# First loads over two queues, a finer start order and the z broadcast through DMA transposes

## Chip, cores and metric

The kernel runs on one core of a Trainium2 chip. The metric is the device time of one execution in microseconds (us); of several executions the median is taken. Engines are named as in the profile: PE is TensorE (PEld its weight loads), DVE VectorE, ACT ScalarE, POOL GpSimd, SP SyncE.

## What is computed

x has 2048 tokens of D = 640 bf16 values. Two branches are mixed by a gate per token:

```python
g = sigmoid((x * gate_w).sum(-1, keepdims=True))
# A: linear attention, 32 heads of 20
q, k, v = heads(x @ wqkv)
pq, pk = phi(q), phi(k)            # phi(t) = where(t > 0, t + 1, exp(t)) + 1e-6
kv = einsum("bhsd,bhse->bhde", pk, v)
z = einsum("bhsd->bhd", pk)        # sum over all tokens
o = einsum("bhqd,bhde->bhqe", pq, kv) / (einsum("bhqd,bhd->bhq", pq, z)[..., None] + 1e-6)
a = merge(o) @ wo
# B: token-shift mixer, then MLP (F = 1728)
h = gelu(layernorm(x) @ w1)        # its four column quarters are shifted by 1, -1, 2, -2 tokens
x1 = x + shifted(h) @ w2
b = x1 + gelu(layernorm(x1) @ w3) @ w4
out = g * a + (1 - g) * b
```

## The kernel before

**Tiles and stages.** The 2048 tokens are 16 tiles of 128; D is five blocks of 128. A matmul needs the contracted dimension on partitions, so x is held as x_tok (tokens on partitions) and as xT (columns of x on partitions). The stages, in TensorE's order: a warm-up of matmuls on constants; q = x wq and k = x wk for the tiles, with phi on ACT and DVE behind them; products of pk and x (GT), from which kv follows; W1, W2 (mixer); W3 with the attention output tiles; W4 and the output. A q or k tile is, for each of five slices k of the weight, a matmul of 512 columns and one of 128 (130 for k, which carries a column of ones and gate_w), into a pair of PSUM banks. I call the two matmuls of tile t and slice k a step (t, k).

**Start.** SyncE's queue issues nearly all first loads one after the other, in program order (lines 676 to 704): x tiles 0 and 1, wq slice 0, x tile 2, wq slices 1 to 4, wk slice 0, x tile 3, wk slices 1 to 4, x tile 4, then DMA transposes of x tiles from 3 on (`x_turn`) and the rest of x. ACT's queue issues only a small load that touches rows of wqkv ("touch") and gate_w. x tiles 0, 1, 2 are turned by TensorE (`t_x`, line 763): five transposes against an identity into one PSUM bank, then one DVE copy of 128x640 to xT. Tile 2's turn also brings gate_w onto partitions with a matmul of 5 columns. The identity is made on GpSimd (line 668) after a memset of ones_c (line 659).

TensorE starts with WARM = 3200 columns of matmuls on ones, turns tiles 0 and 1, adds WARM2 = 512 columns, and goes into `q_three` (line 896), in which the steps of q tiles 0, 1, 2 are interleaved by a list written by hand; (None, None) there is a warm-up of 256 columns and (2, None) the turn of tile 2. `k_two` does the same with k tiles 0 and 1, and from `("k", 2)` on whole tiles follow. `stream` (line 873) emits such a list and takes a pair of banks when a tile's first step comes.

**z.** `z_add` sums pk over the 16 tiles on DVE into zsum (128 partitions x 640), still one partial sum per partition. `zb_group` (line 1025) sums over the partitions and copies the sum to all of them at once: two matmuls with a block of ones as weights (line 600) and zsum as the moving operand, then one DVE copy to zb. `qn_sum` (line 1086) multiplies q tiles by zb for the denominators.

**Order.** Every engine takes its instructions in program order and waits for semaphores that the helper class derives from overlapping tiles. The order of independent pieces ("items") is set by a small planner: each `IT.add(stream, name, duration, function, deps)` is an item with dependences and lags, and `IT.run` repeatedly takes the item that can start first by a cost model kept in the program. So a new item or another modelled cost can move items on all engines. The `ZB` stream's item waits for `("z", 15)` and `("w2", 0)`. On SyncE the DMA transposes of normalised tiles for W1 (`t_xn`, line 849, issued at line 281, sixteen of them), then the loads of w3 and w4 (line 285) follow each other in the same stretch of time.

Of the kernel before, what the change touches and what calls it, by code (L numbers as in the profile page):

```python
# [11 lines left out]
D = 640  # L12
# [404 lines left out]
def _build(nc, A_x, A_wqkv, A_wo, B_w1, B_w2, B_w3, B_w4, gate_w, out, dbg=None, stop=None):  # L417
# [45 lines left out]
    def psb(b, n0, n1):  # L463
        return ps[:, b, :].bitcast(BF16)[:, n0:n1]
# [23 lines left out]
    dnr = pa.alloc("dnr", [128, 2, 4, H], F32)  # L488
    xn = pa.alloc("xn", [128, 3, D], BF16)
# [183 lines left out]
    def dma_in(out_ap, in_ap, key, **kw):  # L673
        return sch.dma("sp", out_ap, in_ap, key, **kw)

    sch.dma("act", junk[0:16, 0, 0:80].rearrange("p (k f) -> p k f", k=KD),
            A_wqkv[:, 0:16].rearrange("(k e r) f -> e r k f", k=KD, r=8)[:, 0, :, :], "touch")
    dma_in(x_tok[:, 0, :], x2[0:128, :], "x0")
    dma_in(x_tok[:, 1, :], x2[128:256, :], "x1")
    def load_wq(k):  # L680
        dma_in(wq[:, k, :], A_wqkv[128 * k:128 * (k + 1), 0:D], "wq%d" % k)

    load_wq(0)
    dma_in(x_tok[:, 2, :], x2[256:384, :], "x2")
    for k in range(1, KD):
        load_wq(k)
    for k in range(KD):
        dma_in(wkg[:, k, 0:D], A_wqkv[128 * k:128 * (k + 1), D:2 * D], "wk%d" % k)
        if k == 0:
            dma_in(x_tok[:, 3, :], x2[384:512, :], "x3")  # L690
# [4 lines left out]
    dma_in(x_tok[:, 4, :], x2[512:640, :], "x4")  # L695
    x_turn(3)
    gwr = xn[:, 1, 0:128]
    dve(lambda e: e.memset(gwr, 0.0), [], [gwr])
    sch.dma("act", xn[0:KD, 1, 0:128], gate_w.rearrange("(k p) -> k p", p=128), "gw")
# [60 lines left out]
    WARM = 3200  # L760
    WARM2 = 512

    def t_x(t):
        b = bank()
        tr_group(b, [x_tok[:, t, 128 * k:128 * (k + 1)] for k in range(KD)])
        src = psb(b, 0, D).rearrange("p (k c) -> p k c", k=KD)
        dst = xT[:, :, 128 * t:128 * (t + 1)]
        if t == 2:
            mm_group(ps[:, b, 448:448 + KD], [(gwr, ident[:, 0:KD])])
        copy(dve, dst, src)  # L770
        if t == 2:
            copy(dve, wkg[:, :, D + 1:D + 2], ps[:, b, 448:448 + KD].rearrange("p (k o) -> p k o", o=1))
# [100 lines left out]
    def stream(order, w, n2, done):  # L873
        bs = {}
        for t, k in order:
# [6 lines left out]
            if k == 0:  # L882
                bs[t] = pair()
                bank_hold.update((bs[t], bs[t] + 1))
# [27 lines left out]
    for i in range(2):  # L912
        addA(("tx", i), 0.28, lambda i=i: t_x(i))
# [414 lines left out]
```

## Time and profile before

| | us |
|---|---|
| median of 8 runs | 260.49 |
| lowest and highest | 260.14, 261.64 |
| profiled execution | 260.24 |
| its span in the profile | 259.0 |
| TensorE busy in it | 256.0 |
| ACT / DVE / POOL busy | 106.5 / 152.1 / 93.5 |
| first real matmul (L889) starts | 5.15 |
| last matmuls end | about 257 |

The span is what the hardware profiler saw of one execution, from its first to its last event. In the groups, "busy" counts every instruction from its start to its modelled end; matmuls are pipelined, so their lengths overlap and 99% busy is not the share of peak. An instruction's line can be that of a helper (line 600 issues most matmuls), so tiles tell more than lines. A wait is put down to the engine whose semaphore came last. "From issue to landing" is the time from the start of a DMA's issue on its queue to its last semaphore step.

### The profile page before, as it was taken

Reading aid. Unit: us, or ns where it says so; the run is one execution under the profiler, and the core shown is the slowest. Engines: PE = TensorE matmul, PEld = TensorE weight load, DVE = VectorE, ACT = ScalarE, POOL = GpSimd, SP = SyncE. Lnnn points to the kernel's source line nnn. Section 1 sums busy time; section 2 is a strip of 40 time slices with the busy share of each in tenths; the row PEclk is TensorE's granted clock in tenths of the full one; section 3 lists DMA queues with packets and bytes.
Section 4 is the critical chain, followed back from the end, with each engine's and each line's share of the span. In section 5 each row is a group of like instructions: output and inputs, shape, how many; then the busy total and the mean of one; then the engine's idle time right before and its main releaser. Section 6 shows DMA issues by size and latency. Waiting matters only on the chain.

```text
span 259.0 us, 4292 instructions
## 1 busy us (share of the span) xinstructions
PE 256.0 (99%) x1685; PEld 132.3 (51%) x1685; DVE 152.1 (59%) x288; ACT 106.5 (41%) x216; POOL 93.5 (36%) x151
## 2 busy tenths in 40 slices
PE   8999999999999999999999999999999999999996
PEld 4555555544454554555445445554455544456453
DVE  1587877899903799998998407992033410143233
ACT  1496777751365766676853240005500045100000
POOL 4013995969962029666914202320011110021001
DMA  6965888682666982552726650232000020000211
GB/s 178 277 131 151 191 172 147 183 128 49 104 127 115 399 284 45 60 101 52 104 50 122 124 70 0 49 90 66 0 3 0 3 101 0 0 3 1 104 51 51
DMA packets 51406, 25.16 MB, mean 97 GB/s; under 512 B 42766, under 2 KB 49975, under 8 KB 51386
## 3 DMA queue, kind: packets, MB, share of 16 engines
q1 hardware_dynamic: 50000, 21.47, 36.6%
q0 software_dynamic: 1136, 3.28, 5.4%
q8 instruction: 13, 0.21, 0.3%
q10 hardware_dynamic: 250, 0.14, 0.2%
q14 instruction: 7, 0.06, 0.1%
HBM read 12.05 MB, written 2.62 MB: 57 GB/s over the span
## 4 chain that ended last, share of the span: by engine, by line
PE 97%; DMA 1%; DVE 1%; SPq 0%; issue 0%
PE ps L600 61%; PE ps L1167 22%; PE ps L796 8%; PE ps L889 2%; DMA wq<-in_A_wqkv_dram 1%; PE ps L1079 1%; PE ps L1149 1%; PE ps L890 1%; DVE x_tok L639 0%; PE ps L969 0%; PE ps L998 0%; SPq L285 0%; DVE xT L665 0%; PE ps L1146 0%; PE ps L611 0%
## 5 line engine op out<-in xcount | busy, mean ns | idle before, releaser
L600 PE MATMUL ps<-xnT,w 128*128 128x512 bf16 x360 | 81.5, 379 | 0.0
L1167 PE MATMUL ps<-w,h2T 128*128 128x512 bf16 (+1 forms) x416 | 58.8, 299 | 0.0
L656 ACT ACTIVATE h2T<-ps 128x512 bf16<-128x512 f32 x52 | 30.5, 598 | 67.5 <-PE ps L600 67.5
L600 PEld LDWEIGHTS ps<-xnT,w 128*128 128x128 bf16 x360 | 34.1, 98 | 38.5 <-issue 0.9
L639 DVE SCALAR_TENSOR_TENSOR x_tok<-ps,stg,abx 128x512 bf16<-128x512 f32 (+1 forms) x32 | 17.3, 550 | 61.5 <-PE ps L1167 61.5
L622 POOL TENSOR_SCALAR abx<-x_tok,stg 128x640 f32<-128x640 bf16 x16 | 15.3, 956 | 98.9 <-DVE x_tok L639 94.9
L1167 PEld LDWEIGHTS ps<-w,h2T 128*128 128x128 bf16 x416 | 32.1, 98 | 24.9 <-issue 1.1
L622 POOL TENSOR_SCALAR xn<-x_tok,st 128x640 bf16<-128x640 bf16 x32 | 34.9, 1099 | 13.8 <-DMA xnT<-xn 13.3
L656 ACT ACTIVATE Er<-ps 128x640 bf16<-128x640 f32 x32 | 22.4, 708 | 16.9 <-PE ps L600 7.9
L655 ACT ACTIVATE junk<-x_tok 128x640 bf16<-128x640 bf16 x32 | 23.7, 739 | 3.1 <-DVE x_tok L637 2.6
L600 PE MATMUL ps<-M_sb,pqnT 128*128 128x512 bf16 (+1 forms) x160 | 24.3, 299 | 0.0
L656 ACT ACTIVATE hsT<-ps 128x512 bf16<-128x512 f32 (+1 forms) x32 | 18.9, 593 | 13.1 <-PE ps L600 12.7
L600 PE MATMUL ps<-w,hsT 128*128 128x512 bf16 (+1 forms) x160 | 23.7, 299 | 0.0
L639 DVE SCALAR_TENSOR_TENSOR abx<-ps,stg,abx 128x640 f32<-128x640 f32 x16 | 14.1, 883 | 12.4 <-PE ps L600 11.3
L600 PE MATMUL ps<-wkg,xT 128*128 128x130 bf16 (+1 forms) x140 | 21.4, 299 | 0.0
L600 PE MATMUL ps<-wq,xT 128*128 128x512 bf16 (+1 forms) x130 | 19.8, 299 | 0.0
L600 PEld LDWEIGHTS ps<-w,hsT 128*128 128x128 bf16 x160 | 13.3, 98 | 12.2
L600 PEld LDWEIGHTS ps<-M_sb,pqnT 128*128 128x128 bf16 x160 | 13.2, 98 | 10.9
L796 PE MATMUL ps<-pk_tok,x_tok 128*128 128x512 bf16 x80 | 17.8, 379 | 0.0
L622 DVE TENSOR_SCALAR Er<-Er 128x640 bf16<-128x640 bf16 x32 | 11.7, 366 | 9.4 <-ACT Er L656 9.3
L1108 DVE TENSOR_TENSOR pq_tok<-pq_tok,dnr 128x300 bf16<-128x300 bf16 (+1 forms) x48 | 16.8, 404 | 0.6
L637 DVE SCALAR_TENSOR_TENSOR x_tok<-ps,x_tok 128x640 bf16<-128x640 f32 x16 | 13.1, 820 | 6.8 <-PE ps L600 5.9
(78 smaller groups left out, 227.9 us busy)
## 6 DMA issues: line engine op xcount, KB each, us to landing
w<-in_B_w_dram SPq DMA_DIRECT2D x1, 2160.0 KB, 9.5
w<-in_B_w_dram SPq DMA_DIRECT2D x1, 2080.0 KB, 15.0
out_dram<-x_tok SPq DMA_DIRECT2D x3, 640.0 KB, 3.1
x_tok<-in_A_x_dram SPq DMA_DIRECT2D x2, 640.0 KB, 5.1
w<-in_B_w_dram POOLq DMA_DIRECT2D x8, 160.0 KB, 4.4
x_tok<-in_A_x_dram SPq DMA_DIRECT2D x5, 160.0 KB, 3.3
wq<-in_A_wqkv_dram SPq DMA_DIRECT2D x5, 160.0 KB, 3.4
wkg<-in_A_wqkv_dram SPq DMA_DIRECT2D x5, 160.0 KB, 4.0
```

Source lines behind the costliest of these rows:

```text
L600: ins = e.matmul(out_ap, l, r, start=(i == 0), stop=(i == n - 1))
L622: return engf(lambda e: e.tensor_scalar(out_ap, in_ap, s1, s2, op0, op1), rd, [out_ap], cost=cost)
L637: return dve(lambda e: e.scalar_tensor_tensor(out_ap, in0, scalar, in1, op0, op1, accum_out=accum), rd, [out_ap, accum], cost=cost + 70.0)
L639: return dve(lambda e: e.scalar_tensor_tensor(out_ap, in0, scalar, in1, op0, op1), rd, [out_ap], cost=cost)
L655: return act(lambda e: e.activation(out_ap, in_ap, func, bias=bias, scale=scale, accum_out=accum), rd, wr, cost=cost)
L656: return act(lambda e: e.activation(out_ap, in_ap, func, bias=bias, scale=scale), rd, wr, cost=cost)
L796: ins = e.matmul(o, l, r, start=(t0 + q_ == 0), stop=(t0 + q_ == NT - 1))
L889: e.matmul(ps[:, b, 0:512], l, w[:, k, 0:512], start=(k == 0), stop=(k == KD - 1))
L890: return e.matmul(ps[:, b + 1, 0:n2], l, w[:, k, 512:512 + n2], start=(k == 0), stop=(k == KD - 1))
L1079: ins = e.matmul(o, l, r, start=st, stop=sp)
L1108: dve(lambda e, o=o, i0=i0, i1=i1: e.tensor_tensor(o, i0, i1, ALU.mult), [i0, dnr[:, 1, sd, :]], [o], cost=cost)
L1167: ins = e.matmul(o, l, r, start=False, stop=(i == KFF - 1), skip_group_check=(n0 > 0))
```

## The change

- x tile 0 and wq slice 0 are each loaded in two column parts, one by SyncE's and one by ACT's queue; wq slices 1, 3, 4 and wk slices 1, 3 are issued by ACT, the rest by SyncE. wq slice 0 is now issued before x tile 1. The touch load is gone. gate_w is loaded by GpSimd's queue, ahead of GpSimd's memsets.
- WARM is 2944 columns and WARM2 256; the warm-up of 256 columns inside `q_three` is gone.
- The turn of tiles 0 and 1 is in two parts with a bank and a copy each: block 0, then blocks 1 to 4. Tile 1 is turned inside `q_three`, after step (0, 0); the order of the steps is another, and tile 2 is turned later in it.
- `stream` takes the pairs of banks of all its tiles at its start.
- zb is made without TensorE: a DMA transpose of zsum into zb (`z_turn`), a DVE sum along the free dimension into zc and an ACT copy that spreads zc over zsum (`z_rows`), and a second DMA transpose into zb (`z_back`). The item `("zt",)` waits for `("t1", 7)`, `("zr",)` for the first kv group.

```diff
@@ -486,6 +486,7 @@
     M_sb = pa.alloc("M_sb", [128, KD, D], BF16)
     zb = pa.alloc("zb", [128, D], BF16)
     dnr = pa.alloc("dnr", [128, 2, 4, H], F32)
+    zc = pa.alloc("zc", [128, KD], F32)
     xn = pa.alloc("xn", [128, 3, D], BF16)
     junk = pa.alloc("junk", [128, 1, D], BF16)
     qprod = pa.alloc("qprod", [128, D], F32)
@@ -673,30 +674,39 @@
     def dma_in(out_ap, in_ap, key, **kw):
         return sch.dma("sp", out_ap, in_ap, key, **kw)
 
-    sch.dma("act", junk[0:16, 0, 0:80].rearrange("p (k f) -> p k f", k=KD),
-            A_wqkv[:, 0:16].rearrange("(k e r) f -> e r k f", k=KD, r=8)[:, 0, :, :], "touch")
-    dma_in(x_tok[:, 0, :], x2[0:128, :], "x0")
-    dma_in(x_tok[:, 1, :], x2[128:256, :], "x1")
-    def load_wq(k):
-        dma_in(wq[:, k, :], A_wqkv[128 * k:128 * (k + 1), 0:D], "wq%d" % k)
-
-    load_wq(0)
-    dma_in(x_tok[:, 2, :], x2[256:384, :], "x2")
-    for k in range(1, KD):
-        load_wq(k)
-    for k in range(KD):
-        dma_in(wkg[:, k, 0:D], A_wqkv[128 * k:128 * (k + 1), D:2 * D], "wk%d" % k)
-        if k == 0:
-            dma_in(x_tok[:, 3, :], x2[384:512, :], "x3")
+    def load_x(t):
+        dma_in(x_tok[:, t, :], x2[128 * t:128 * (t + 1), :], "x%d" % t)
+
+    def load_wq(k, queue):
+        sch.dma(queue, wq[:, k, :], A_wqkv[128 * k:128 * (k + 1), 0:D], "wq%d" % k)
+
+    def load_wk(k, queue):
+        sch.dma(queue, wkg[:, k, 0:D], A_wqkv[128 * k:128 * (k + 1), D:2 * D], "wk%d" % k)
 
     def x_turn(t):
         sch.dma("sp", xT[:, :, 128 * t:128 * (t + 1)], x_tok[:, t, :], "trx%d" % (t % 4), transpose=True)
 
-    dma_in(x_tok[:, 4, :], x2[512:640, :], "x4")
-    x_turn(3)
     gwr = xn[:, 1, 0:128]
     dve(lambda e: e.memset(gwr, 0.0), [], [gwr])
-    sch.dma("act", xn[0:KD, 1, 0:128], gate_w.rearrange("(k p) -> k p", p=128), "gw")
+    for n0, n1, queue in ((0, 384, "sp"), (384, D, "act")):
+        sch.dma(queue, x_tok[:, 0, n0:n1], x2[0:128, n0:n1], "x0", group_total=2)
+    for n0, n1, queue in ((0, 320, "sp"), (320, D, "act")):
+        sch.dma(queue, wq[:, 0, n0:n1], A_wqkv[0:128, n0:n1], "wq0", group_total=2)
+    load_x(1)
+    load_wq(1, "act")
+    load_wq(2, "sp")
+    load_wq(3, "act")
+    load_x(2)
+    load_wq(4, "act")
+    load_wk(0, "sp")
+    load_wk(1, "act")
+    load_x(3)
+    load_wk(3, "act")
+    load_wk(2, "sp")
+    load_wk(4, "sp")
+    load_x(4)
+    x_turn(3)
+    sch.dma("pool", xn[0:KD, 1, 0:128], gate_w.rearrange("(k p) -> k p", p=128), "gw")
     for c in range(1, NCH):
         t0 = 5 if c == 1 else 4 * c
         dma_in(x_tok[:, t0:4 * c + 4, :], x2[128 * t0:512 * (c + 1), :].rearrange("(n p) d -> p n d", p=128), "xc%d" % c)
@@ -757,19 +767,18 @@
         assert tags.get((buf, sl)) == what, ("stale ring slot", buf, sl, what, tags.get((buf, sl)))
 
     IT = _Items()
-    WARM = 3200
-    WARM2 = 512
+    WARM = 2944
+    WARM2 = 256
 
     def t_x(t):
-        b = bank()
-        tr_group(b, [x_tok[:, t, 128 * k:128 * (k + 1)] for k in range(KD)])
-        src = psb(b, 0, D).rearrange("p (k c) -> p k c", k=KD)
-        dst = xT[:, :, 128 * t:128 * (t + 1)]
-        if t == 2:
-            mm_group(ps[:, b, 448:448 + KD], [(gwr, ident[:, 0:KD])])
-        copy(dve, dst, src)
-        if t == 2:
-            copy(dve, wkg[:, :, D + 1:D + 2], ps[:, b, 448:448 + KD].rearrange("p (k o) -> p k o", o=1))
+        for k0, k1 in ((0, 1), (1, KD)) if t < 2 else ((0, KD),):
+            b = bank()
+            tr_group(b, [x_tok[:, t, 128 * k:128 * (k + 1)] for k in range(k0, k1)])
+            if t == 2:
+                mm_group(ps[:, b, 448:448 + KD], [(gwr, ident[:, 0:KD])])
+            copy(dve, xT[:, k0:k1, 128 * t:128 * (t + 1)], psb(b, 0, 128 * (k1 - k0)).rearrange("p (k c) -> p k c", k=k1 - k0))
+            if t == 2:
+                copy(dve, wkg[:, :, D + 1:D + 2], ps[:, b, 448:448 + KD].rearrange("p (k o) -> p k o", o=1))
 
     def phi(b, dst, after_exp=None):
         se = slot("E", 3)
@@ -872,6 +881,9 @@
 
     def stream(order, w, n2, done):
         bs = {}
+        for t in sorted({t for t, k in order if k is not None}):
+            bs[t] = pair()
+            bank_hold.update((bs[t], bs[t] + 1))
         for t, k in order:
             if k is None:
                 if t is None:
@@ -879,9 +891,6 @@
                 else:
                     t_x(t)
                 continue
-            if k == 0:
-                bs[t] = pair()
-                bank_hold.update((bs[t], bs[t] + 1))
             b = bs[t]
             l = xT[:, k, 128 * t:128 * (t + 1)]
 
@@ -894,8 +903,8 @@
                 done(t, b)
 
     def q_three():
-        order = [(0, 0), (None, None), (1, 0), (2, None), (0, 1), (1, 1), (2, 0), (0, 2), (1, 2), (2, 1), (0, 3), (0, 4),
-                 (1, 3), (2, 2), (1, 4), (2, 3), (2, 4)]
+        order = [(0, 0), (1, None), (0, 1), (1, 0), (1, 1), (0, 2), (1, 2), (2, None), (0, 3), (1, 3), (0, 4), (2, 0),
+                 (2, 1), (1, 4), (2, 2), (2, 3), (2, 4)]
         stream(order, wq, 128, lambda t, b: phi(b, pq_tok[:, t + 1, :]))
 
     def k_out(t, b):
@@ -909,8 +918,7 @@
         IT.add("A", name, dur, fn, deps)
 
     addA(("warm",), 0.0, lambda: warmup(WARM, 0.834))
-    for i in range(2):
-        addA(("tx", i), 0.28, lambda i=i: t_x(i))
+    addA(("tx", 0), 0.28, lambda: t_x(0))
     addA(("warm", 1), 0.0, lambda: warmup(WARM2, 0.42))
     addA(("q", 2), 4.08, q_three)
     addA(("k", 1), 2.72, k_two)
@@ -1022,18 +1030,27 @@
         for j in range(KD):
             sch.dma("sp", M_sb[60:68, j, :], Mt[8 * j:8 * j + 8, :], "mt", group_total=KD)
 
-    def zb_group():
-        b = pair()
-        mm_group(ps[:, b, 0:512], [(ones_c[:, 0:128], zsum[:, 0:512])])
-        mm_group(ps[:, b + 1, 0:128], [(ones_c[:, 0:128], zsum[:, 512:D])])
-        copy(dve, zb[:, :], psf[:, 512 * b:512 * b + D])
+    zT = zb[:, :].rearrange("p (k n) -> p k n", n=128)
+    zrep = zsum[:, :].rearrange("p (k n) -> p k n", n=128)
+
+    def z_turn():
+        sch.dma("sp", zT, zsum[:, :], "trz", transpose=True)
+
+    def z_rows():
+        dve(lambda e: e.tensor_reduce(zc[:, :], zT, mybir.AxisListType.X, ALU.add), [zT], [zc[:, :]], cost=820.0)
+        activation(zrep, zc[:, :].unsqueeze(2).to_broadcast([128, KD, 128]), ACTF.Copy)
+
+    def z_back():
+        sch.dma("sp", zT, zsum[:, :], "trz", transpose=True)
 
     IT.add("KVF", ("kvt", 1), 0.0, kvt_group, deps=[(("g", KD - 1), 1.0)])
     IT.add("KVF", ("lt", 1), 0.0, lt_evac, deps=[(("kvt", 1), 0.0)])
     IT.add("KVF", ("m", 0), 0.0, m_last, deps=[(("lt", 1), 1.0), (("w1", 2, 2), 0.0)])
     IT.add("KVF", ("m", 1), 0.0, m_first, deps=[(("lt", 1), 1.0), (("w3", 0, 5), 0.0)])
     IT.add("MT", ("mt",), 0.0, m_tail, deps=[(("m", 1), 1.5), (("qt", 2), 0.0)])
-    IT.add("ZB", ("zb",), 0.0, zb_group, deps=[(("z", NT - 1), 1.7), (("w2", 0), 0.0)])
+    IT.add("ZB", ("zt",), 0.0, z_turn, deps=[(("z", NT - 1), 1.7), (("t1", 7), 0.0)])
+    IT.add("ZB", ("zr",), 0.0, z_rows, deps=[(("zt",), 2.6), (("kvt", 1), 0.0)])
+    IT.add("ZB", ("zb",), 0.0, z_back, deps=[(("zr",), 1.5)])
 
     SHIFT = (1, -1, 2, -2)
     PIECES = [[(0, 128, SHIFT[j])] for j in range(4)] + [[(32 * g_, 32 * (g_ + 1), SHIFT[g_]) for g_ in range(4)]]
```

## Prediction

> **What bounds the kernel now.** First the page's parts 1 and 4.
>
> ```profile
> PE 256.0 (99%) x1685; PEld 132.3 (51%) x1685; DVE 152.1 (59%) x288; ACT 106.5 (41%) x216; POOL 93.5 (36%) x151
> ...
> PE 97%; DMA 1%; DVE 1%; SPq 0%; issue 0%
> ```
>
> TensorE is the bound. The share hides the start, so next the waits of its weight loads (us in total, times, longest), in the stretch 5.2 to 257 us:
>
> ```profile
> PEld ps L1149 <- ACT h2T L656: 1.3, 3, 0.4
> ...
> PEld ps L889 <- DMA wq<-in_A_wqkv_dram: 0.6, 1, 0.6
> PEld ps L889 <- DVE xT L665: 0.4, 1, 0.4
> ```
>
> Weight loads run ahead of matmuls, so a wait of theirs need not stop the array: where the load waits on ACT at L1149 the matmuls still follow each other without a hole. Spacing the matmul starts by their columns leaves only two holes after 5 us: before the first real matmul (5.15) and 0.22 us at 6.88. After 6.88 TensorE never stands. So a microsecond saved at the start, or a matmul removed, shortens the run one for one, unless a new hole opens. The chain of waits has the start in order:
>
> ```profile
> 0.79 0.40 SPq L285
> 1.25 0.42 SPq L285
> 1.71 3.39 DMA wq<-in_A_wqkv_dram
> 5.15 0.39 PE ps L889
> ...
> 6.33 0.50 DVE xT L665
> 6.88 0.39 PE ps L889
> ```
>
> The first real matmul waits for wq slice 0, the third load that SyncE issues. TensorE's timeline shows what stands before it:
>
> ```profile
> 0.83 2.83 PE L862 MATMUL ps<-const-bfloat16-1.0 128*128 128x512 bf16 x7 [0.83 <-PEq L1313]
> 3.45 1.27 PE L611 MATMUL ps<-ident,x_tok 128*128 128x128 bf16 x10
> 4.52 0.57 PE L862 MATMUL ps<-const-bfloat16-1.0 128*128 128x512 bf16 x1
> 5.15 0.39 PE L889 MATMUL ps<-wq,xT 128*128 128x512 bf16 x1
> ```
>
> Ten transposes start 0.107 us apart, 4.52 less 3.45; later ones 0.054. The array runs at half pace. The 512-column warm-up matmul takes 0.63 us at half pace and 0.38 at full; the one at 4.52 took 0.57, so it turned fast about three quarters through, near 4.85 us.
>
> **What the Trainium skill says.** "TensorE: Matmul & The Clock Gate", Part 1: the array starts at half clock and goes to full after a busy window of about 3.4 us, whose phase is free. Here it took 0.83 to 4.85, 4.0 us: agrees, and a first matmul before 4.85 is paid double. "DMA: Bandwidth & Descriptors", "Issuing engines are not separate DMA queues": a second issuing engine saves only issue time. Here an issue takes 0.43 us and a landed slice about 0.45 (0.16 MB at the 369 GB/s of the stretch 7.0 to 7.5), so issue is not the limit, and I count mainly on the changed order. The trace doesn't show two full queues at once.
>
> **The change part by part.**
>
> *Loads.* From issue to landing, by window: x tiles 0 and 1 2.4 us, wq slice 0 3.4, x tile 2 and wq slice 1 3.3. So they land at 3.2, 3.65, 5.1, 5.5 and 5.95. A slice should cost 0.45; slice 0 came 1.45 after x tile 1. The stretches 3.0 to 4.0 show only 102 and 138 GB/s with DMA engines 0.7 busy: slow packets. Slice 0 moves ahead of x tile 1: 0.45 earlier, 4.65. What two queues do in the slow spell is not shown: nothing (4.65), or the second fills it so that slice 0 is ready when TensorE is free, about 4.0 (end of its first transposes and warm-up). I take 0.3 earlier, 4.35. Halves cut rows of 1280 bytes to 512 to 768; the trace has 18 ns for 256 bytes and 55 for 1280, so two halves of 640 cost some 64 ns instead of 55: with eight rows per engine, 0.07 us per slice, inside that choice. The touch load (2.3 us, ACT) goes; whether it speeds slice 0 isn't shown, 0 to 0.4 us of loss, taken at 0, kept in the range.
>
> *ACT's queue* issues seven loads, 0.4 us each, from 0.80 to about 4.0; behind them stand the table load (1.28 us, at 1.85 now) and the first Exp, which waits for TensorE until 8.72. Hidden by 3 us.
>
> *gate_w on GpSimd.* Later GpSimd issues take 0.5 to 1.1 us, and this one waits for the VectorE memset (0.88, 0.11). The memset of ones_c and the identity are behind it: identity ready at 1.89 now, then at 2.6 to 3.2. The first transpose comes at 3.24 (next point). Cost 0, at worst 0.1. gate_w itself is needed at x tile 2's turn, after 6.5; GpSimd loads later take 4.4 to 6.8 us at the median, so it is there at about 6 at the latest but for 1 us in the worst case, kept in the range.
>
> *Warm-up.* 256 columns less at half pace: 0.21, transposes from 3.24. Five transposes 0.53, 256 columns 0.21: TensorE is free at 4.0, before slice 0.
>
> *Q order.* Before, from 5.15 to K tile 2 at 12.62 is 7.47 us: 25 steps (640 columns, 0.272 each) 6.80, 256 warm-up columns 0.11, x tile 2's turn and gate matmul 0.34, the hole 0.22. After: 6.80 + 0.34 + x tile 1's turn 0.28 = 7.42, without warm-up and hole (three steps now lie between x tile 2's copy, 0.49, and its use). Starting at 4.35, 0.5 us to the fast clock count half: as if started at 4.60.
> New holes: x tile 1 lands 0.45 after slice 0 (4.80), step (0,0) ends about 4.87: none. wq slice 1 at 5.25, x tile 1's turn ends 5.15: 0.10. Five steps bring it to 6.61; x tile 2 is the fifth slice after wq slice 0, 4.35 + 2.25 = 6.60, or later by the slow spell that wq slice 3 shows now (3.5 to 3.7 us to landing instead of 3.3): 0.15 taken, 0 to 0.6. So K tile 2 starts at 4.60 + 7.42 + 0.25 = 12.27 instead of 12.62: **0.35 us gained**. The split copy of x tiles 0, 1 adds two VectorE instructions of 0.1 to 0.2 us while VectorE idles (3.2 us of waiting there): 0. Pairs of PSUM banks taken up front leave two banks for turns; the copies free these within 0.5 us: 0.
>
> *z.* Two matmuls of 640 columns on ones and zsum go:
>
> ```profile
> L600 PE MATMUL ps<-zsum,ones_c x2: 219/299/379, 83.2 to 83.4; 128*128 128x512 bf16 x1, 128*128 128x128 bf16 x1
> ```
>
> Those are pipelined lengths; at 0.4167 ns a column they hold TensorE 0.272 us (83.22 to 83.49). **0.27 gained.** The VectorE copy (CAST, 0.82) goes, a reduction comes (the TENSOR_REDUCE of 640 elements, 0.82): 0. ACT gets a copy of 640 columns, 0.7 us like the 128x640 ACTIVATE; it idles 0.27 to 1.84 us between GELUs there: hidden. SyncE gets two DMA transposes, 1.28 us of issue and 2.6 to landing each, in a row that is full:
>
> ```profile
> 68.16 13.80 SPq L281 DMA_TRANSPOSE xnT<-xn  x10
> 82.01 8.34 SPq L285 DMA_DIRECT2D w<-in_B_w_dram  x4
> ```
>
> The first waits for zsum (ready 71.64), behind tile 7's transpose (69.58 to 71.24): 0.4 lost. It lands by 74.3. The reduction stands at the latest behind the Lt multiplies (77.64 to 78.6), ends 79.4, ACT's copy about 80.8; the second transpose waits for it, and xn tiles 12 to 15 and the w3, w4 loads wait behind that on SyncE: 2.6 of issue and up to 2.7 of waiting, 5.3 us. Tile 15 then lands at 83.3 + 5.3 = 88.6; its reader, the sixteenth W1 group, starts at 97.2; w3 (landing about 97) is first read near 112. Eight us of cover. zb is ready at 83.5 to 86 (84.5 now), read first at 85.8 by VectorE, whose next PSUM reads would stand behind it; TensorE has other banks for some 5 us: 0.
>
> **Sum.** 0.35 + 0.27 = 0.62. The profiled execution took 260.24 (span 259.0 and 1.24 around it), so 259.6 of its kind; it lies 0.25 under the median 260.49 of the runs shown, and 260.49 less 0.62 is **259.9**.
>
> **Rivals.** *Two queues overlap fully:* wq slice 0 at 4.0, as if started at 4.43, no holes: 4.43 + 7.42 = 11.85, 0.77 gained, with z 1.04: 259.45. For: DMA engines are not full in the slow spell. Against: the sharing of 16 engines.
> *Supply-bound:* slice 0 at 4.65 (as if 4.75), x tile 2 late by 0.6 and slice 1 by 0.2: K tile 2 at 12.97, 0.35 lost, with z 0.08 slower: 260.6. For: the bytes before x tile 2 now include wq slices 2 and 3.
> *Slower: the clock.* TensorE idles from 4.0 to slice 0, in the window that now ends at 4.85 fully busy. If the hole makes the gate refuse that window, another 3.4 us (the skill's window, estimate) run at half pace: 1.7 lost, less 0.25 of holes that vanish: 261.3. It decides once the hole is too large a share of the window; the 0.2 us hole now lies behind the switch, so the trace cannot say. Against: 0.35 of 3.4 us is a tenth.
> *z late:* if ACT's copy sits before GELUs while the reduction waits, or zb lands past 91, PSUM fills: about 261.5. Against: the eight us above.
>
> **How the numbers follow.** Forecast 0.50 (259.5 to 260.3), full overlap 0.28 (259.2 to 259.7), supply-bound 0.10 (to 260.8), clock 0.06, z late 0.06. Measurement tells 0.3%, 0.78 us: faster is under 259.71, slower over 261.27. Faster: 0.28 and 0.10 of the forecast's lower edge, 0.38. Slower: 0.06 + 0.06 = 0.12. Same: 0.50. The range 259.2 to 260.8 holds forecast, supply-bound and nearly all of overlap.
>
> **What would show it.** First L889 matmul at 4.35 (4.0 overlap, 4.65 supply-bound); K tile 2's matmuls from 12.27; full pace from near 4.85, or 8.2 for the clock rival; no zsum matmuls, and the W1/W2 stretch free of holes. A hole of TensorE after 13 us, or a first step later than 4.9, would make the forecast wrong.

## The result, and the profile after

| | before | after |
|---|---|---|
| median, us | 260.57 (31 runs) | 265.88 (11 runs) |
| lowest and highest | 260.11, 261.64 | 264.63, 267.05 |
| profiled execution | 260.24 | 264.95 |
| its span | 259.0 | 263.7 |
| TensorE busy | 256.0 | 255.9 |
| K tile 2 starts (first matmul behind the start) | 12.62 | 12.95 |

The changed kernel is slower: ratio 1.0197 with a 95% interval of 1.0181 to 1.0212. I had predicted 259.9 (259.2 to 260.8). In what follows, lines of the changed kernel are those of its own file: the helper that issues most matmuls is now L601, the turns of x tiles L612, the first steps L898 and L899.

The page's parts 1 and 4 of the kernel after:

```profile
PE 255.9 (97%) x1683; PEld 131.7 (50%) x1683; DVE 151.9 (58%) x290; ACT 107.4 (41%) x217; POOL 94.0 (36%) x152
...
PE 78%; DMA 12%; SPq 5%; DVE 4%; issue 0%; ACT 0%
```

TensorE's busy time has not grown, and its share fell from 99 to 97%. So the time is in holes. That its share of the chain fell from 97 to 78% overstates them: a hole of 0.28 us at 41.8 leads the chain back into the first 41 us of loads and transposes of x, and loads of x alone are 8.4% of it; the second z transpose is 1.6%. The waits (us in total, times, longest) name who waits and who ends the wait:

```profile
DVE zc L1040 <- DMA zb<-zsum: 5.3, 1, 5.3
...
DVE qprod L631 <- DMA zb<-zsum: 4.6, 1, 4.6
...
PE ps L601 <- DVE x_tok L638: 1.9, 1, 1.9
...
PE ps L1006 <- ACT hsT L657: 1.2, 1, 1.2
...
PE ps L601 <- DVE dnr L623: 1.0, 1, 1.0
...
PE ps L612 <- DMA x_tok<-in_A_x_dram: 0.7, 1, 0.7
```

The last line is a hole in the start. The three PE lines above it are holes of TensorE from 90 to 99 us, and their releasers stand behind the wait of qprod for the second z transpose. The chain of waits joins them (start, length, what):

```profile
78.21 5.79 PE ps L601 x30
84.03 0.10 ACT hsT L657
84.13 4.25 DMA zb<-zsum
88.41 0.83 DVE qprod L631
89.26 0.82 DVE dnr L1106
```

Why the second z transpose is issued as late as 84.13 stands in SyncE's timeline (start, length, queue, number), which answers to the two lines shown of before, where ten xn transposes were followed directly by the w3 and w4 loads:

```profile
63.11 11.73 SPq L281 DMA_TRANSPOSE xnT<-xn  x8
74.88 1.28 SPq L281 DMA_TRANSPOSE zb<-zsum  x1
76.20 7.89 SPq L281 DMA_TRANSPOSE xnT<-xn  x6
84.13 1.28 SPq L281 DMA_TRANSPOSE zb<-zsum  x1
85.46 9.10 SPq L285 DMA_DIRECT2D w<-in_B_w_dram  x4
```

ACT's copy that it needs ran from 80.13 to 80.86:

```profile
80.13 0.73 ACT L657 ACTIVATE zsum<-zc 128x640 bf16<-128x640 f32 x1
```

So the second transpose could have been issued at 80.86. It was put behind the last of the xn transposes, was issued 3.3 us later, and took 4.3 us to land, where the first took 2.6. The w3 loads follow it directly, but they followed the last xn transpose of the kernel before too, and that one took 2.6; why this one took longer is not shown. VectorE's timeline shows who waited, and what stood behind:

```profile
83.70 0.08 DVE L638 DVE_READ_ACCUMULATOR x_tok<-ps,x_tok 128x1 f32 x1
88.41 0.82 DVE L631 TENSOR_TENSOR qprod<-pq_tok,zb 128x640 f32<-128x640 bf16 x1 [4.62 <-DMA zb<-zsum]
89.26 0.82 DVE L1106 TENSOR_REDUCE dnr<-qprod 128x32 f32<-128x640 f32 x1
90.00 0.81 DVE L638 SCALAR_TENSOR_TENSOR x_tok<-ps,x_tok 128x640 bf16<-128x640 f32 x1
```

The last of these reads the second W2 tile out of PSUM. In order of program it is behind qprod, so it waits with it, and each further W2 read (90.00, 93.81, 97.61) comes behind 3.0 us of normalising q. Before, the second W2 read stood ahead of the first qprod, as VectorE's timeline of the kernel before shows:

```profile
85.05 0.82 DVE L637 SCALAR_TENSOR_TENSOR x_tok<-ps,x_tok 128x640 bf16<-128x640 f32 x1 [0.53 <-PE ps L600]
...
85.80 0.82 DVE L630 TENSOR_TENSOR qprod<-pq_tok,zb 128x640 f32<-128x640 bf16 x1
```

TensorE, which fills PSUM banks meanwhile, then stands in the changed kernel:

```profile
90.97 1.52 PE L601 MATMUL ps<-w,hsT 128*128 128x512 bf16 x10 [1.03 <-DVE dnr L623]
...
96.12 0.46 PE L1006 MATMUL ps<-wo_aug,Lt 60*64 60x512 bf16 x6 [1.19 <-ACT hsT L657]
98.49 1.25 PE L601 MATMUL ps<-xnT,w 128*128 128x512 bf16 x5 [1.91 <-DVE x_tok L638]
```

Brackets count from a matmul's modelled end. Counted from the matmul starts by their columns, as in the prediction, the three holes are 1.19, 1.36 and 2.07, together 4.62 us. The start, last:

```profile
4.25 0.61 PE L898 MATMUL ps<-wq,xT 128*128 128x512 bf16 x1
4.65 0.27 PE L899 MATMUL ps<-wq,xT 128*128 128x128 bf16 x1
5.66 0.45 PE L612 MATMUL ps<-ident,x_tok 128*128 128x128 bf16 x5 [0.74 <-DMA x_tok<-in_A_x_dram]
```

The first step begins 0.9 us earlier than before (4.25 instead of 5.15), then TensorE waits 0.96 us for x tile 1. K tile 2 starts 0.33 later than before. Sum: 4.62 and 0.33, 0.28 of a hole at 41.8 (below), less 0.27 for the two matmuls that are gone, is 4.96; the spans differ by 4.7.

### The profile page after: what moved, and what is told of

Its sections match the earlier page's. It is cut to its first block, busy times and chain, and to the rows that moved or that the text cites. A ratio compares the mean times of both kernels' runs of the same rounds, so it can differ in the third digit from the quotient of the medians.

```text
span 263.7 us, 4292 instructions
## 1 busy us (share of the span) xinstructions
PE 255.9 (97%) x1683; PEld 131.7 (50%) x1683; DVE 151.9 (58%) x290; ACT 107.4 (41%) x217; POOL 94.0 (36%) x152
## 4 chain that ended last, share of the span: by engine, by line
PE 78%; DMA 12%; SPq 5%; DVE 4%; issue 0%; ACT 0%
PE ps L601 47%; PE ps L1184 21%; DMA x_tok<-in_A_x_dram 8%; PE ps L805 7%; SPq L281 4%; DMA xT<-x_tok 2%; DMA zb<-zsum 2%; SPq L285 1%; DVE dnr L1106 1%; DVE qprod L631 1%; PE ps L1096 1%; DVE x_tok L638 1%; PE ps L1166 1%; DVE pq_tok L1125 1%; DVE x_tok L640 0%
## 5 line engine op out<-in xcount | busy, mean ns | idle before, releaser
L601 PE MATMUL ps<-xnT,w 128*128 128x512 bf16 x360 | 81.5, 379 | 1.9 <-DVE x_tok L638 1.9
L601 PEld LDWEIGHTS ps<-xnT,w 128*128 128x128 bf16 x360 | 34.2, 98 | 40.4 <-DVE x_tok L638 2.2
L623 POOL TENSOR_SCALAR abx<-x_tok,stg 128x640 f32<-128x640 bf16 x16 | 14.8, 924 | 99.9 <-DVE x_tok L640 94.9
L601 PE MATMUL ps<-w,hsT 128*128 128x512 bf16 (+1 forms) x160 | 23.7, 299 | 1.0 <-DVE dnr L623 1.0
L601 PE MATMUL ps<-M_sb,pqnT 128*128 128x512 bf16 (+1 forms) x160 | 24.3, 299 | 0.0
L601 PE MATMUL ps<-wkg,xT 128*128 128x130 bf16 (+1 forms) x140 | 21.4, 299 | 0.0
L601 PEld LDWEIGHTS ps<-w,hsT 128*128 128x128 bf16 x160 | 13.2, 98 | 13.5 <-issue 1.5
L601 PE MATMUL ps<-wq,xT 128*128 128x512 bf16 (+1 forms) x130 | 19.8, 299 | 0.1
L601 PEld LDWEIGHTS ps<-M_sb,pqnT 128*128 128x128 bf16 x160 | 13.2, 98 | 10.8
L631 DVE TENSOR_TENSOR qprod<-pq_tok,zb 128x640 f32<-128x640 bf16 x16 | 14.1, 881 | 4.6 <-DMA zb<-zsum 4.6
L1125 DVE TENSOR_TENSOR pq_tok<-pq_tok,dnr 128x300 bf16<-128x300 bf16 (+1 forms) x48 | 15.7, 380 | 0.6
```

The lines of the kernel that those rows point to most:

```text
L601: ins = e.matmul(out_ap, l, r, start=(i == 0), stop=(i == n - 1))
L623: return engf(lambda e: e.tensor_scalar(out_ap, in_ap, s1, s2, op0, op1), rd, [out_ap], cost=cost)
L631: return engf(lambda e: e.tensor_tensor(out_ap, a, b_, op), [a, b_], [out_ap], cost=cost)
L1125: dve(lambda e, o=o, i0=i0, i1=i1: e.tensor_tensor(o, i0, i1, ALU.mult), [i0, dnr[:, 1, sd, :]], [o], cost=cost)
```

## The experiments

Two theories stood against each other from here. Main theory: the z step costs what it costs because of its second transpose's place on SyncE and the wait at the head of VectorE's order, behind which its PSUM reads stand; the start is a loss of some tenths. Rival: the start, through the clock, or the new z chain wherever it is put. The start and the z step were first taken apart. Ratios are to the kernel before, whose median was 260.42 to 260.51 beside these runs.

**e1, the changed kernel with z made by the two matmuls again: the new start alone.**

```diff
-    def z_turn():
...
-    IT.add("ZB", ("zb",), 0.0, z_back, deps=[(("zr",), 1.5)])
+    def zb_group():
...
+    IT.add("ZB", ("zb",), 0.0, zb_group, deps=[(("z", NT - 1), 1.7), (("w2", 0), 0.0)])
```

> The changed kernel with zb made by the two matmuls on ones again, so the new start alone. Main theory (z chain stands in SyncE's queue, VectorE stands behind it, TensorE has three holes of 4.6 us together): the holes at 91 to 99 us are gone; what is left is the start, K tile 2 at 12.9 instead of 12.6 and the 0.28 us hole at 41.8, so 260.6 to 261.2. Rival (the start carries more than its first 13 us show, through other landing times later): 262 or more.

Measured: 262.22 (260.40 to 262.89, 17 runs), ratio 1.0050 (1.0032 to 1.0068). The holes between 90 and 100 us are gone, so these belong to z. But the total is far above what I expected, and the runs fall in two groups: six from 260.40 to 260.88, eleven from 261.89 to 262.89, with 1.8 us between the groups' medians. The profiled run, 262.89, is one of the upper group. Its TensorE timeline in the start:

```profile
4.09 0.39 PE L898 MATMUL ps<-wq,xT 128*128 128x512 bf16 x1
4.32 0.22 PE L899 MATMUL ps<-wq,xT 128*128 128x128 bf16 x1
6.39 0.45 PE L612 MATMUL ps<-ident,x_tok 128*128 128x128 bf16 x5 [1.85 <-DMA x_tok<-in_A_x_dram]
...
6.95 0.38 PE L898 MATMUL ps<-wq,xT 128*128 128x512 bf16 x1
...
7.76 0.63 PE L898 MATMUL ps<-wq,xT 128*128 128x512 bf16 x1
...
10.45 0.62 PE L898 MATMUL ps<-wq,xT 128*128 128x512 bf16 x1
...
10.96 0.38 PE L898 MATMUL ps<-wq,xT 128*128 128x512 bf16 x1
```

A 512-column matmul takes 0.38 us at full pace and 0.63 at half. The array is at full pace from about 4.1, stands 2.02 us for x tile 1 (landed at 6.34), works at full pace to 7.5, and is at half pace from there to 10.9. The granted clock of the same trace (the number before the last two of each line, averaged over the stretch that the line begins with) says so too:

```profile
7.00:8.00 1.00, 1.00 (x7) 0.41 (x6) 0.30 (x1) 0.00 (x0) 0.00 (x0) 0.75 1.07 379
...
10.00:11.00 1.00, 1.00 (x7) 0.45 (x5) 0.21 (x2) 0.00 (x0) 0.00 (x0) 0.54 0.10 34
```

From 4.1 to 7.5 and from there to 10.9 are 3.4 us each, the length of the clock gate's window in the Trainium skill ("TensorE: Matmul & The Clock Gate", Part 1). So in this run a window with 2.02 us of hole in it was followed by one at half pace, which costs 1.7 us, about the distance of the groups. K tile 2 starts at 15.33, 2.7 later than before. This is my clock rival, but of another hole and another window than the ones I had weighed.

It does not explain the whole group. Each run's granted clock is on record: it is 0.993 in three of the eleven slower runs (the profiled one and those of 262.74 and 262.88) and 1.000 in the other eight. That does not clear the clock in those eight, since the figure is 1.000 also for the profiled runs of e4 and e8 below, whose matmuls go at half pace to about 9.9: half pace before the first rise is not in it. Which of the two, or what else, made the eight slow is not shown.

**e2, the kernel before with the new z alone.**

```diff
-    def zb_group():
...
-    IT.add("ZB", ("zb",), 0.0, zb_group, deps=[(("z", NT - 1), 1.7), (("w2", 0), 0.0)])
+    def z_turn():
...
+    IT.add("ZB", ("zb",), 0.0, z_back, deps=[(("zr",), 1.5)])
```

> The kernel before with the new z chain alone. Main theory: holes of some 4.6 us as in the changed kernel, less 0.27 for the two matmuls: 264.6 to 265.3. Rival (the z chain misses its readers only because the start moved everything): 260.3 to 261.

Measured: 265.62 (264.41 to 266.07, 4 runs), ratio 1.0187 (1.0162 to 1.0213). Nearly the whole loss, with the start of before. The instructions that touch zb, in its profile:

```profile
L281 SPq DMA_TRANSPOSE zb<-zsum x2: 1276/1276/1276, 75.7 to 84.9; - x2
...
  DVE qprod L631: 4.4, 1
```

The second transpose is issued at 84.9, VectorE waits 4.4 us, and TensorE's holes are 0.93, 1.36 and 2.07 at 91.5, 96.6 and 99.0. So the z step is shown to be the cause of nearly the whole loss. A further hole of 1.25 at 42.6 is in this profile; it is taken up under what stays open.

**e3, the changed kernel with the second z transpose ahead of the last xn transposes.** One dependence more makes the eleventh xn transpose wait for it; nothing else is changed.

```diff
-t_xn(1, u), deps=[(("n1", u), 1.1)])
+t_xn(1, u), deps=[(("n1", u), 1.1)] + ([(("zb",), 0.0)] if u == 10 else []))
```

> The changed kernel with the transpose of xn tile 10 made to follow the second z transpose, so that SyncE issues it six transposes earlier; VectorE's order is the same. Main theory: SyncE waits for ACT's copy until about 80.9, zb lands at about 83.5 instead of 88.4, before VectorE asks for it at about 84 to 86; no hole over 0.3 us in 88 to 100; 260.6 to 261.2. Rival (VectorE has too much work between the W2 tiles once zb's place in its order has moved, late or not): holes of 1 us and more stay, 262.5 or more.

Measured: 261.04 (260.47 to 264.36, 22 runs), ratio 1.0034 (1.0018 to 1.0050). SyncE's timeline:

```profile
73.39 1.27 SPq L281 DMA_TRANSPOSE zb<-zsum  x1
74.70 1.27 SPq L281 DMA_TRANSPOSE xnT<-xn  x1
80.88 1.20 SPq L281 DMA_TRANSPOSE zb<-zsum  x1
82.12 9.21 SPq L281 DMA_TRANSPOSE xnT<-xn  x6
91.38 7.21 SPq L285 DMA_DIRECT2D w<-in_B_w_dram  x4
```

The transpose is issued at 80.88, as soon as ACT's copy is done, and lands at 83.5. VectorE's timeline at the same place:

```profile
83.69 0.08 DVE L638 DVE_READ_ACCUMULATOR x_tok<-ps,x_tok 128x1 f32 x1
83.69 0.82 DVE L631 TENSOR_TENSOR qprod<-pq_tok,zb 128x640 f32<-128x640 bf16 x1
```

No wait, and TensorE has no hole from 80 to 100: 4.8 us come back by the place of one DMA in a queue. The main theory's step is shown. What the place costs is shown too: SyncE stands from 75.97 to 80.88, the w3 and w4 loads begin at 91.38 instead of 82.01, and run beside the transposes of the second normalisation, which start at 101. The first three of these took 4.7 to 5.5 us to land, where the first three took 2.6 before. There TensorE has a new hole of 0.47 at 110.25, waiting for such a transpose. That is more than the 0.27 that the two matmuls were worth.

**e4, the changed kernel with qprod later on VectorE.** The place of the transpose stays; the first qprod waits for three W2 reads, so that these don't stand behind it.

```diff
         deps = [(("zb",), 1.0), (("q", max(t, 2)), 2.0)]
+        if t < 7:
+            deps.append((("w2", t + 2), 1.0))
```

> The changed kernel with the first readers of zb moved behind later W2 tiles: on VectorE three PSUM reads of W2 tiles stand ahead of the first product with zb instead of one; the orders of SyncE and TensorE are the same. Main theory: zb lands at 88.4 as before but VectorE doesn't stand for it (under 0.5 us instead of 4.6), no hole over 0.3 us in 88 to 100; 260.6 to 261.3. Rival (it is the transposes' own traffic or SyncE's delay of xn tiles 10 to 15 that TensorE waits for): the holes stay, 264 or more.

Measured: 263.05 (261.86 to 263.30, 6 runs), ratio 1.0091 (1.0073 to 1.0109). The total misses, and the z part does not. VectorE:

```profile
84.73 0.82 DVE L638 SCALAR_TENSOR_TENSOR x_tok<-ps,x_tok 128x640 bf16<-128x640 f32 x1 [3.20 <-PE ps L601]
...
87.17 0.82 DVE L638 SCALAR_TENSOR_TENSOR x_tok<-ps,x_tok 128x640 bf16<-128x640 f32 x1 [1.61 <-PE ps L601]
...
90.69 0.82 DVE L638 SCALAR_TENSOR_TENSOR x_tok<-ps,x_tok 128x640 bf16<-128x640 f32 x1 [2.69 <-PE ps L601]
...
91.44 0.82 DVE L631 TENSOR_TENSOR qprod<-pq_tok,zb 128x640 f32<-128x640 bf16 x1
```

The transpose is issued at 86.4, later even than in the changed kernel, and nobody waits for it; between 85 and 100 TensorE has one hole of 0.15. So a late zb costs next to nothing by itself: it costs because PSUM reads are queued behind its reader. And e3, in which the reader stands where it does in the changed kernel, shows that this order costs nothing by itself either: it takes both. In the profiled run, the 263 come from the start, where the array was at half pace until 9.8, with a hole of 1.32 us behind the first step (K tile 2 at 15.02, 2.40 later than before), and from a hole of 0.69 at 127.8, in which TensorE waits for ACT. 259.0 and 2.40, 0.69, 0.15, less 0.27, is 261.97; the span was 262.0.

**e5, the kernel before with the new z in e3's place.** This is e2 with e3's line, with the start of before, so that the clock stays out.

```diff
-t_xn(1, u), deps=[(("n1", u), 1.1)])
+t_xn(1, u), deps=[(("n1", u), 1.1)] + ([(("zb",), 0.0)] if u == 10 else []))
```

> The start of the kernel before, with the new z chain and its second transpose ahead of xn tile 10's: the z part as it was meant. Main theory: no hole in 80 to 100 us, the two matmuls' 0.27 us are saved: 260.0 to 260.4. Rival (the chain still costs something, in holes of VectorE's or SyncE's making): 260.7 or more.

Measured: 260.39 (259.96 to 261.56, 13 runs), ratio 0.9998 (0.9988 to 1.0009). No gain of the z step in the better place shows: in the profile 0.27 us of matmuls are gone, and a hole of 0.18 at 109.45 and 0.10 of a later K tile 2 take it back. The interval still leaves room for a gain of 0.3 us.

**e10, the kernel before without the touch load.** One of my bounds was that its absence makes wq slice 0 up to 0.4 us later.

```diff
-    sch.dma("act", junk[0:16, 0, 0:80].rearrange("p (k f) -> p k f", k=KD),
-            A_wqkv[:, 0:16].rearrange("(k e r) f -> e r k f", k=KD, r=8)[:, 0, :, :], "touch")
```

> The kernel before without the small touch load of wqkv. If the touch warms what wq slice 0 needs, slice 0 lands at 5.6 or later instead of 4.8 to 5.1, and 260.9 to 261.4; if not, it lands at 4.8 to 5.3 and 260.2 to 260.7. In the second case the lost touch is no part of the changed kernel's slower start.

Measured: 260.27 (259.84 to 260.96, 12 runs), ratio 0.9996 (0.9984 to 1.0008); slice 0 landed at 5.12, before at 5.10. No effect of the touch load shows here.

**e8 and e9, the start with other orders of loads.** Both are e3 with another start. e8 issues x tile 1 before wq slice 0; e9 leaves the order and issues all on SyncE.

```diff
+    load_x(1)
     for n0, n1, queue in ((0, 320, "sp"), (320, D, "act")):
         sch.dma(queue, wq[:, 0, n0:n1], A_wqkv[0:128, n0:n1], "wq0", group_total=2)
-    load_x(1)
```

and, in e9, every "act" among the first loads becomes "sp", as in

```diff
-    load_wq(1, "act")
+    load_wq(1, "sp")
     load_wq(2, "sp")
-    load_wq(3, "act")
+    load_wq(3, "sp")
```

> The early-zb kernel with x tile 1 issued before SyncE's half of wq slice 0. A slow spell of packets stands at 3.0 to 4.4 us in all traces; main theory: it hits whatever is third on a queue. Then x tile 1 lands by 4.2 instead of 5.6 to 6.3, wq slice 0 at 4.8 to 5.4 instead of 4.2, the first step starts there and there is no hole after it: 260.2 to 260.8. Rival (x's second tile is slow because of its own rows): x tile 1 still lands after 5.3.

> The early-zb kernel with all first loads on SyncE's queue, in the changed order; TensorE's order is the same. Sharing theory (in the slow spell wq slice 1 on ACT's queue takes engine time from x tile 1): x tile 1 lands 0.4 us or more earlier, at 4.9 to 5.2, the hole shrinks under 0.7: 260.3 to 260.9. Rival (the spell alone sets it): x tile 1 lands at 5.5 or later, 260.9 to 261.4.

Measured: e8 261.67 (260.47 to 263.57, 21 runs), ratio 1.0049 (1.0034 to 1.0064); e9 261.95 (261.28 to 262.25, 5 runs), ratio 1.0053 (1.0040 to 1.0066). When each load had landed, in us of each profile:

| | x tile 0 | wq slice 0 | x tile 1 | wq slice 1 | K tile 2 starts |
|---|---|---|---|---|---|
| before | 3.24 | 5.10 | 3.60 | 5.91 | 12.62 |
| after | 3.17 | 4.21 | 5.62 | 5.82 | 12.95 |
| e3 (same start as after) | 3.31 | 3.68 | 5.89 | 6.11 | 13.23 |
| e8 | 3.14 | 5.34 | 3.81 | 5.58 | 15.02 |
| e9 | 3.16 | 4.47 | 5.03 | 5.50 | 13.81 |

In these five, two loads land by 3.1 to 4.5 and the third between 5.0 and 5.9, whichever it is. Moving wq slice 0 forward makes x tile 1 the third, and the work needs both. Why the third is so late is only in part shown. Some packets are slow: of the 88 to 217 packets of 1280 bytes that start between 3.0 and 4.4 us in these profiles, 6 to 20 take 200 ns or more, up to 1422, and the others mostly 55. But from 3.0 to 4.0 the DMA engines move 102 to 210 GB/s in four of the five and about 300 in e8, whose third load is no earlier, so a slow spell that hits whatever is third is not shown. The number of queues shows better. In the seven profiles of this document with their first loads of x, wq and wk on SyncE's queue alone (before, e2, e5, e6, e9, e10, e12) the third load lands at 4.64 to 5.12, in the seven with two queues (after, e1, e3, e4, e7, e8, e11) at 5.13 to 6.34, and there the other queue's wq slice 1 lands within 0.25 us behind it.

My expectations on the landings held (e8's x tile 1, e9's x tile 1 0.9 earlier than e3's), and those on the times missed. In e8 the hole lies before the first step instead of behind it, and in the profiled run the array stayed at half pace to about 10, as in e4. In e9 x tile 1 comes earlier and wq slice 2 later (7.28, a hole of 0.71), and in the profiled run the array came to full pace at about 5.9 instead of 4.75.

**e7 and e11, the hole of the start filled with warm-up matmuls.** If the upper group is the clock's, it must vanish when the array is kept busy while x tile 1 is awaited. e7 is e3, e11 is e1, both with six warm-ups of 256 columns after step (0, 0).

```diff
-        order = [(0, 0), (1, None), (0, 1), (1, 0), (1, 1), (0, 2), (1, 2), (2, None), (0, 3), (1, 3), (0, 4), (2, 0),
+        order = [(0, 0)] + 6 * [(None, None)] + [(1, None), (0, 1), (1, 0), (1, 1), (0, 2), (1, 2), (2, None), (0, 3), (1, 3), (0, 4), (2, 0),
```

> The early-zb kernel with six warm-up matmuls of 256 columns after step (0, 0), so that TensorE works while x tile 1 is awaited. Its runs without them spread from 260.5 to 264.4. Clock theory (the hole at 4.9 to 6 us falls into a window of the clock gate in some executions, and the next 3.4 us then go at half pace, 1.7 us lost): the spread goes, all runs within 0.8 us of the fastest, median 260.5 to 261.0. Rival (the spread is x tile 1's own landing time): median and spread stay, 261.0 and 2 us.

> The new start with the old z (whose 17 runs fell in two groups, 260.4 to 260.9 and 261.9 to 262.9), with six warm-up matmuls of 256 columns after step (0, 0), in the hole in which x tile 1 is awaited. Clock theory (the hole puts the array back to half pace for one window of 3.4 us in those runs in which it fills enough of a window: 1.7 us): the upper group is gone, nothing over 261.7, median 260.7 to 261.2. Rival (the groups come from x tile 1's landing or from later stages): both groups stay, median over 261.8.

Measured: e7 263.06 (262.63 to 264.94, 6 runs), ratio 1.0112 (1.0087 to 1.0138), a miss. The start has no hole and no second stretch at half pace (K tile 2 at 13.33), but new holes of 0.83 at 94.9 and 1.26 at 111.9 came, in the stretches of the q normalising and of the w3 loads; qprod took 1.33 us at 88.1 instead of 0.82, beside GpSimd's normalising. This run can't separate the two, so I repeated it without the new z. e11: 261.14 (260.55 to 262.27, 22 runs), ratio 1.0029 (1.0020 to 1.0038). The start in its profile:

```profile
4.51 0.31 PE L899 MATMUL ps<-wq,xT 128*128 128x128 bf16 x1
4.62 1.49 PE L871 MATMUL ps<-const-bfloat16-1.0 128*128 128x128 bf16 x12
5.89 0.61 PE L612 MATMUL ps<-ident,x_tok 128*128 128x128 bf16 x5
6.34 0.38 PE L898 MATMUL ps<-wq,xT 128*128 128x512 bf16 x1
```

Full pace comes late here (about 6.2), and stays. Of e1's 17 runs, 11 are above 261.7; of e11's 22, 3 are, and the values form one group. No run of e11 has a granted clock under 1.000. The median fell by 1.1 us although work of no use was added; the intervals of the two ratios just overlap, and the two were measured on different chips, each beside the kernel before. This supports the hole, through the clock, as the cause of e1's upper group and does not prove it; with 3 runs still above 261.7 it isn't all of the spread.

**e12 and e6, is there something to keep?** e12 is the kernel before without the warm-up between the first steps, and with steps (0, 2) and (1, 2) ahead of (2, 0); e6 is the same with e5's z.

```diff
-        order = [(0, 0), (None, None), (1, 0), (2, None), (0, 1), (1, 1), (2, 0), (0, 2), (1, 2), (2, 1), (0, 3), (0, 4),
+        order = [(0, 0), (1, 0), (2, None), (0, 1), (1, 1), (0, 2), (1, 2), (2, 0), (2, 1), (0, 3), (0, 4),
```

> The kernel before with two edits of TensorE's order only: the warm-up of 256 columns inside the q steps is gone (0.11 us), and steps (0, 2) and (1, 2) come before (2, 0), so that x tile 2's copy is done in time (0.22 us). Loads and z as before. Theory (what moves from the start's end goes through one for one): K tile 2 at 12.3 instead of 12.6, 260.05 to 260.25. Rival (a later wait takes it back, as TensorE is now ahead of loads): 260.4 to 260.6.

> The old start with the same two edits of the order, and the new z chain with its second transpose ahead of xn tile 10's. If the parts add: 0.33 from the order, and what the early z chain gave alone (0.0, its 0.27 being taken back by a hole near 110 us): 260.0 to 260.2.

Measured: e12 260.31 (259.92 to 260.64, 14 runs), ratio 0.9990 (0.9982 to 0.9999): the lowest ratio found, 0.1% below the kernel before. Its interval hardly excludes 1, it is the best of twelve versions, and e10, which only lacks the touch load, has a lower median (260.27), so I don't call it a gain. It is less than I expected. In its profiled run K tile 2 came at 12.85, not at 12.3: the array was at half pace to about 5.9 instead of 4.85, and TensorE waited 0.23 us for wq slice 2 (landed at 7.06). e6: 260.40 (260.05 to 260.73, 14 runs), ratio 0.9997 (0.9990 to 1.0005): a miss; in its profile half pace lasted to about 6.0 and that wait was 0.56 us.

**Does the account close?** For each profile, its span less the 259.0 of before, beside the sum of three things read from its matmul starts: K tile 2's start less 12.62, the holes after it, and less 0.27 where the two z matmuls are gone.

| | K tile 2 | later holes | matmuls | sum | span |
|---|---|---|---|---|---|
| after | 0.33 | 4.90 | -0.27 | 4.96 | 4.7 |
| e1 | 2.71 | 0 | 0 | 2.71 | 2.7 |
| e2 | 0.12 | 5.61 | -0.27 | 5.46 | 5.3 |
| e3 | 0.61 | 0.47 | -0.27 | 0.81 | 0.8 |
| e4 | 2.40 | 0.84 | -0.27 | 2.97 | 3.0 |
| e5 | 0.10 | 0.18 | -0.27 | 0.01 | 0.0 |
| e6 | 0.57 | 0.18 | -0.27 | 0.48 | 0.5 |
| e7 | 0.71 | 2.09 | -0.27 | 2.53 | 2.4 |
| e8 | 2.40 | 0.76 | -0.27 | 2.89 | 2.8 |
| e9 | 1.19 | 0.16 | -0.27 | 1.08 | 1.0 |
| e10 | 0.03 | 0 | 0 | 0.03 | 0.0 |
| e11 | 0.71 | 0.39 | 0 | 1.10 | 1.1 |
| e12 | 0.23 | 0 | 0 | 0.23 | 0.2 |

It closes to 0.13 us but for the kernel after (0.26) and e2 (0.16), which have the largest holes. The medians do not simply add: e1 is 1.71 and e2 5.11 above the kernel before, after 5.31. Two things make the sum too high: e2's profiled run holds the hole of 1.25 at 42.6, and e1's median lies in its upper group, while 4 of after's 11 runs (264.63 to 265.05) lie apart from the other 7 (265.64 to 267.05). How often each occurs is not settled by 4 and 11 runs. The clock has a part in it: three of after's runs (265.64, 266.37, 267.05) and two of e2's four (265.71, 266.07) have a granted clock of 0.994, which is some 3.2 us at half pace. e2 has the start of before, and no run of the kernel before beside these experiments is under 1.000, so the holes of the z step, 1.36 and 2.07 us within 4.5 us, may cost the clock as well as their own length. No trace of such a run was kept, so this is not shown.

## Why the prediction was wrong

**The z step is what failed.** The prediction gave it "0.27 gained" and nothing on the other side: "zb is ready at 83.5 to 86 (84.5 now), read first at 85.8 by VectorE, whose next PSUM reads would stand behind it; TensorE has other banks for some 5 us: 0". The runs showed 4.62 us of holes in its place, and 5.11 us by the median of e2, which has the new z alone. Four things in it can be held against the runs.

- *The place on SyncE was assumed.* I let the second transpose follow ACT's copy at once, and counted what would wait behind it. The planner put it behind all sixteen xn transposes. With the assumed place (e3) zb landed at 83.4, the early end of what I wrote; with the real one at 88.4. The first transpose was placed late as well: zsum was ready at 72.3, and it was issued at 74.88 and landed at 77.5, not by 74.3. That cost nothing, since ACT's copy still ended at 80.86, where I had 80.8 by another route. The diff alone does not show this; it shows that the order is the outcome of modelled times, and my text on the kernel said that a new item can move others. I should have carried both places, and priced the late one.
- *The late case was named and mis-sized.* The rival "z late" was there with 261.5 and a chance of 0.06. The holes took 4.62 us, where 261.5 leaves about 1.6 over the forecast of 259.9, since I asked only when zb "lands past 91". It landed at 88.4 and it hurt: VectorE's order had changed too, and the first qprod was next at 83.7, ahead of the second W2 read, where before it came behind it at 85.8. A reader's old start is not the time from which it blocks.
- *"Other banks for some 5 us" ended the account too early.* TensorE did have banks for some 6 us (from 83.7 to 89.8, where the first hole begins), and I stopped there. But VectorE was 4.6 us behind when zb landed, had 3.0 us of q normalising between one W2 read and the next, and so could not catch up: all three holes came after zb had landed, and the two larger ones last, ending at 96.1 and 98.5. With three W2 reads ahead of that reader (e4), holes of 0.15 us were left of the 4.62.
- *The cover for the loads was thinner than said.* "w3 (landing about 97) is first read near 112. Eight us of cover": even with the early place the loads began 9.4 us (e3) or 7.9 us (e5) later, not 5.3, and a hole of 0.47 (e3) or 0.18 (e5) came near 110. In e3 TensorE waited there for a transpose of xn, not for w3; the likely reason is that w3's bytes now ran beside those transposes. I had asked when the moved load is needed, not what it would meet.

The other terms of this step hold: an issue of 1.28 us each, 0.82 for the reduction, 0.73 for ACT's copy, 2.6 to landing for the first transpose, and 0.27 for the two matmuls, which e5's profile shows as gained and lost again.

**The start: first step right, next load wrong.** The first step was predicted at 4.35 and came at 4.25. "x tile 1 lands 0.45 after slice 0 (4.80)": it landed at 5.62, so the gain of 0.35 became a loss of 0.33. I had read the low rate from 3.0 to 4.0 as wq slice 0's misfortune; in every order that was tried the third load was the late one. The rival "full overlap" was even right about its own load in other executions (wq slice 0 at 3.80 and 3.68, the first step at 4.09 and 4.05 in e1 and e3), and wrong that no hole follows (2.02 and 1.62). As the Trainium skill says in "DMA: Bandwidth & Descriptors", "Issuing engines are not separate DMA queues", the queues interleave on the same engines. The traces agree: with a second queue filled, the third load landed at 5.13 to 6.34, with one at 4.64 to 5.12 (5.89 in e3 and 5.03 in e9, which differ in this alone). I had used that page only for what a second queue saves, not for what it takes from the load that is needed first. "Supply-bound" gave K tile 2 at 12.97 and it came at 12.95, but by another load than the x tile 2 and wq slice 1 that it named, so that agreement is luck. gate_w on GpSimd, the split copies, ACT's issues and the missing touch load cost nothing that the traces show, as predicted; the first transpose came at 3.36 and not 3.24, behind which TensorE still had to wait for wq slice 0.

**The clock rival was right in kind.** I had put its hole before the first step and gave it 0.06 and 1.7 us. In e1 the hole came behind the first step, and the price was 1.7 us in the profiled run. In e8's profiled run it was the case that I had described: a hole before the first step, with the array still at half pace, and half pace to about 10. In the profiled run of the changed kernel itself the clock stayed full after a hole of 0.96, so in that run the rival cost nothing.

**Open.** The hole of 0.28 at 41.8 (1.25 at 42.6 in e2, 0.39 at 45.3 in e11): in the changed kernel's trace a load of x took 8.1 us to land beside GpSimd's loads of w1 (7.5 in e2, 6.0 before, 6.4 in e1), and the transposes behind it were late. It is missing in e1, e3, e4 and e5, so I take it for chance, and this was not tried. What makes the third load late even with one queue, and some packets slow, was not found; the touch load is not it (e10).

## What to carry to other kernels

Before work is moved from the bound engine to a chain over other engines, find the place of every link in its in-order queue, and price the worst place that the planner could choose; then look at what is queued behind the reader of the result, since a late operand costs by what stands behind it (4.6 us of waiting became 4.6 us of holes, and 0.15 when three PSUM reads went first). A DMA that is pushed back is asked two things, when it is needed and what it will run beside. At a kernel's start, an earlier first matmul is worth nothing by itself: the first two or three operands together set the pace, and a hole right behind the first step can cost half a clock window (1.7 us in e1) more than its own length.

## What the runs showed of the hardware

- A hole of 2.02 us was followed by 3.4 us at half pace (e1); holes of 0.96 (after) and 1.62 (e3) were not. Where the array was still at half pace, it stayed so to 9.8 us with a hole of 1.32 (e4). The Trainium skill's advice on "TensorE: Matmul & The Clock Gate", "Why this matters for your kernels", is to avoid idle gaps of over about 3 us; here less than that was dear, and the measurement decides. These are single traces, so they bound the limit and don't fix it.
- With the first matmul at 0.83 us in every profile, full pace came at 3.7 (e3), 4.1 (e1), 4.75 (after), 4.85 (before), 5.9 (e9, e12) and 6.2 us (e7, e11), so a kernel's start is paid differently from one execution to the next.
- A DMA transpose of 128x640 bf16 mostly took 2.6 us to landing, and 3.7 to 5.5 in some cases: the second z transpose 4.3 (after), 3.9 (e2) and 3.7 (e4), those that ran beside w3's and w4's bytes 4.7 to 5.5 (e3).
- With the first loads on two queues the third one landed at 5.13 to 6.34 us, with one queue at 4.64 to 5.12 (seven profiles each).
- VectorE's product of 128x640 took 1.33 us instead of 0.82 where GpSimd was normalising tiles at the same time (e7 at 88.1).
